# Attention with expert routing on one core: the first queries, a spread of maxima, a float32 key tile and a gate's transposes

## The chip, the cores and the metric

The kernel runs on one core of one Trainium2 chip. The metric is the device time of one execution in microseconds (us). TensorE is PE in the rows, its weight loads PEld, VectorE DVE, ScalarE ACT, GpSimd POOL and SyncE, which issues most transfers, SP.

## The reference

Attention with pooled queries, then a mixture of experts on its output. The routing is sequential over the tokens of a batch: a token keeps its predecessor's expert where a local gate says so.

```python
# q, k, v: (4, 8, 1152, 64) float32
q_pool = q.reshape(B, H, S // 2, 2, D).mean(axis=3)            # 576 queries a head
scores = scale * np.matmul(q_pool, k.transpose(0, 1, 3, 2))
scores = scores - np.max(scores, axis=-1, keepdims=True)
attn = np.exp(scores)
attn = attn / (np.sum(attn, axis=-1, keepdims=True) + 1e-09)
x = np.matmul(attn, v)                       # heads side by side: (4, 576, 512)
logits = x @ w_gate                          # 8 experts; local = sigmoid(x @ w_local)
e = argmax(logits) if s == 0 or local < 0.5 else e_of_the_token_before
out[b, s] = softmax(logits)[e] * (np.maximum(x @ w1[e], 0.0) @ w2[e])
```

## The kernel before

The 32 heads (4 batches of 8) are worked in 16 **pairs**, and each head in 9 **steps**, one for each tile of 128 keys: 288 steps `s`, 18 in a pair. Numbers are split into a high and a low 16-bit part, and products of the parts are added up in PSUM. The loop over `s` in `attention` writes the instructions in the order in which each engine runs them (the schedule is manual); what follows is what one turn of it issues.

- `scores(s)`: four products of 288 queries each (L227, L229) into a buffer `sc` (there are two), then one exponential on ScalarE (L231) into `ph`, float32.
- `feed_max(s)`: the maxima of the scores, which every exponential of a head needs ahead. A **unit** is a product of 512 or 128 columns into a buffer `psm` (L199, L201, L193; there are two) and a reduction of it on VectorE (L203, L194). An even head has 12 units (three of them, on the tile `QD`, for both heads' last 64 queries), an odd head 9. The list `when` sets the step from which a unit is issued: for head `n` it begins 13 steps before the head and ends within 9. After a head's last unit VectorE takes the maxima over units (L207), TensorE transposes them (L216), and ScalarE writes them as one row of `QA` (L217).
- `low(g)`: the low part of the exponentials, `ph` minus its upper half (L243), on GpSimd for even steps and for key tile 4 of a head, on VectorE for the other odd steps.
- `av(s - 6)`: the product with the values, six steps later. Where `F32K` names the key tile, it is five float32 products (L267), and there is no `low`; otherwise fifteen 16-bit ones (L269 to L271). `F32K` names tile 8 of every head and tile 4 of every odd head.
- `prep_ops(p)`: nine steps that make the 16-bit parts of pair p's keys, queries and values, spread over the steps from the 13th of pair p - 2: `kd` (L124, ScalarE), `qf` (L130, GpSimd), `qh` (L135, ScalarE), `kl` (L147) and `ql` (L153, GpSimd), `vt` (L163 ScalarE, L166 GpSimd), with transfers on SP that copy them to their places (`ks`, `qd`, `qs`, `qa`). Each SP transfer waits for its data at the head of one queue, in order. `load(p)` fetches `qf`, `kf` and `vf` of a pair into single buffers.
- `extra(s)`: weights of the experts. `WSTEPS` are 16 steps; 8 before one a transfer, 2 before it the high part (L526, ScalarE), at it the low part (L532, VectorE).
- After a batch's last head comes its **gate**, one small operation a step from the list `slow`: five transfers that transpose the attention output (`tr`, L562, on SP), the products of the logits (`logits2`, L600, TensorE), a chain of small VectorE operations (L606 to L703), and for batch 2 also `full_ops`. Between two transposes stand `nop` steps. An operation with a set of steps beside it waits until `s % 18` is in the set; for batch 2 that is `GPL2`, all but 4 and 8.

The start: pair 0 is prepared with some steps on VectorE (`first`), the units of head 0 are issued one after the other, each with a product whose result is not used (`warm`, L94), and then the loop begins. A copy of the last 64 queries of both heads into `QD` stands on VectorE there (L139). The preparation of pair 1 is issued from step 0 on, two operations a step. After the 288 steps come the last gate, the routing and eight phases of expert products.

```python
if first:
    V.tensor_copy(QD[i][r, r], qh[r, 512:576])          # L139
...
w = n * NKT - NKT - LEAD + (k * NKT) // nu              # L284, NKT 9, LEAD 4, nu 12 or 9
...
ts = [x for t in range(5) for x in [lambda t=t: tr(t, 8)] + [nop] * (NOP2 if b == B - 2 else 3)]   # L716, NOP2 2
```

## Time and profile before

| | us |
|---|---|
| median of three runs | 700.83 |
| lowest and highest | 698.24, 702.76 |
| the profiled execution | 698.33 |
| its span in the trace | 696.3 |

The profiled execution lies 2.5 us below the median, and 2.0 us of it lie around the span. Within the span the first exponential starts at 26.6 us, the 288 steps end near 438, and the rest is the last gate, the routing and the experts. A pair's stretch is counted below from the start of its first exponential to that of the next pair's. A row of a stretch has its bounds, its length, the busy time of PE, PEld, DVE, ACT and POOL with the number of instructions, the granted TensorE clock (1.00 is 2.4 GHz, 0.50 is 1.2 GHz), the busy share of the transfer engines and GB/s; the five rows of the first group are the pairs 0, 1, 3, 11 and 13.

### The profile page before, as it was taken

What the parts mean: (1) busy time and instruction counts of PE and PEld (TensorE: products, weight loads), DVE (VectorE), ACT (ScalarE), POOL (GpSimd) and SP (SyncE); (2) the same over time, 40 slices, a digit from 0 to 9 for tenths busy, and PEclk for the clock granted to TensorE, in tenths of its full rate; (3) what the DMA queues carried; (4) which work ended last, traced back from release to release, by engine and by line L of the source; (5) the groups of instructions that cost most, each with busy time, mean ns of one, the idle gap of its engine ahead of it and who ended that gap; (6) DMA issues with size and microseconds to landing.
All of it is one profiled execution on the core that took longest, in us unless ns stands there. A gap on an engine that the chain in (4) does not pass through costs nothing.

```text
span 696.3 us, 22820 instructions
## 1 busy us (share of the span) xinstructions
PE 647.7 (93%) x9214; PEld 504.7 (72%) x9214; DVE 594.8 (85%) x1084; ACT 426.7 (61%) x833; POOL 387.8 (56%) x346
## 2 busy tenths in 40 slices
PE   3799999999999999999997999979999999999994
PEld 0378778878888888887885778868649848848941
DVE  7778999999999999999986998578758899899952
ACT  2357777787776786777774666439785634643500
POOL 7477977977977887787794844558100000000073
PEclk9989999999999999999999999999999999999997
DMA  7365545648635748556574500838678877976762
GB/s 228 108 178 178 138 124 173 172 114 210 186 81 196 214 109 204 169 149 177 163 133 131 152 4 14 207 96 304 199 257 285 307 259 257 322 270 224 271 252 107
DMA packets 84221, 127.48 MB, mean 183 GB/s; under 512 B 37135, under 2 KB 43407, under 8 KB 84112
## 3 DMA queue, kind: packets, MB, share of 16 engines
q1 hardware_dynamic: 80912, 115.92, 55.1%
q0 software_dynamic: 3200, 10.05, 4.2%
q8 instruction: 76, 1.25, 0.7%
q14 instruction: 33, 0.27, 0.1%
HBM read 69.05 MB, written 10.04 MB: 114 GB/s over the span
## 4 chain that ended last, share of the span: by engine, by line
PE 46%; issue 27%; DVE 13%; DMA 4%; POOL 3%; ACT 3%; SPq 2%; POOLq 0%; DVEq 0%; ACTq 0%
PE sc L227 8%; PE sc L229 8%; PE psm L201 6%; PE av L267 6%; DVE mx L203 4%; PE av L270 4%; PE av L271 4%; PE av L269 4%; POOL out L1131 3%; DVE pl L243 2%; PE psm L199 1%; DVE w L532 1%; PE psh L216 1%; DMA xT<-xr 1%; DVE qd L139 1%
## 5 line engine op out<-in xcount | busy, mean ns | idle before, releaser
L231 ACT ACTIVATE ph<-sc 128x576 f32<-128x576 f32 x288 | 186.7, 649 | 101.5 <-PE sc L229 74.6
L203 DVE TENSOR_REDUCE mx<-psm 128x1 f32<-128x512 f32 (+1 forms) x300 | 193.1, 660 | 23.4 <-PE psm L201 21.5
L243 POOL TENSOR_TENSOR pl<-ph 128x576 f16<-128x576 f32 x128 | 174.6, 1374 | 15.1 <-ACT ph L231 15.1
L270 PE MATMUL av<-vt,ph 128*128 128x64 f16 x1200 | 136.0, 196 | 0.0
L269 PE MATMUL av<-vt,ph 128*128 128x65 f16 x1200 | 135.4, 193 | 0.0
L271 PE MATMUL av<-vt,pl 128*128 128x65 f16 x1200 | 135.1, 192 | 0.0
L243 DVE TENSOR_TENSOR pl<-ph 128x576 f16<-128x576 f32 x112 | 127.7, 1140 | 2.0 <-ACT ph L231 2.0
L270 PEld LDWEIGHTS <-ph 128*128 128x128 bf16 x1200 | 112.4, 98 | 21.9 <-issue 0.6
L269 PEld LDWEIGHTS <-ph 128*128 128x128 bf16 x1200 | 113.6, 98 | 16.6 <-issue 8.4
L227 PE MATMUL sc<-qs,ks 128*128 128x288 f16 x576 | 118.8, 288 | 0.8 <-ACT ph L231 0.7
L229 PE MATMUL sc<-qa,ks 65*128 65x288 f16 (+1 forms) x576 | 118.9, 288 | 0.3 <-ACT qa L217 0.3
L271 PEld LDWEIGHTS <-pl 128*128 128x128 f16 x1200 | 112.9, 100 | 0.0
...
L1127 PE MATMUL pso<-w,hq 128*128 x480 | 107.5, 380 | 0.0
L532 DVE SCALAR_TENSOR_TENSOR w<-wf,w 128x512 f16<-128x512 f32 x128 | 94.7, 747 | 13.8 <-ACT w L526 13.5
L201 PE MATMUL psm<-ks,qs 128*128 128x512 f16 x248 | 90.0, 384 | 7.3 <-DVE mx L203 7.2
L1116 PEld LDWEIGHTS <-wc 128*128 128x128 f16 x1728 | 87.7, 98 | 6.2 <-issue 4.4
L526 ACT ACTIVATE w<-wf 128x512 f16<-128x512 f32 x128 | 78.8, 631 | 18.8 <-DMA wf<-wq 17.9
L1127 PEld LDWEIGHTS <-hq 128*128 128x128 f16 (+1 forms) x576 | 45.8, 102 | 59.8 <-issue 11.7
L1116 PE MATMUL psh<-xr,wc 128*128 128x128 f16 (+1 forms) x1584 | 84.0, 211 | 2.3 <-DVE wc L984 1.1
L1225 POOL TENSOR_TENSOR xr<-xf,xr 128x320 f16<-128x320 f32 x30 | 35.5, 1182 | 61.1 <-PE sc L229 46.7
L229 PEld LDWEIGHTS <-ks 65*128 65x128 f16 (+1 forms) x576 | 56.8, 99 | 15.6 <-issue 0.6
...
## 6 DMA issues: line engine op xcount, KB each, us to landing
wf<-wq SPq DMA_DIRECT2D x128, 256.0 KB, 4.4
...
```

What stands on the lines that cost most here:

```text
L201: T.matmul(m[:, 0:w], q[:, t * 128:t * 128 + 128], k[:, c * 512:c * 512 + w], start=True, stop=True)
L203: V.tensor_reduce(out=mx[:, i, c:c + 1], in_=m[:, 0:w], op=ALU.max, axis=AX.X)
L227: T.matmul(sc[:, c, 0:288], ksl, QS[p][:, j, c * 288:(c + 1) * 288], start=True, stop=False)
L229: T.matmul(sc[:, c, 0:288], kal, QA[p % 3][u, j, c * 288:(c + 1) * 288], start=False, stop=True)
L231: A.activation(out=PHI[g % NPH][:, r * Q:(r + 1) * Q].rearrange("p (c q) -> p c q", c=2), in_=sc[:, :, 0:288], func=AF.Exp, scale=1.0 / 16)
L243: x.tensor_tensor(out=PLO[g % NPH][:, r * Q:r * Q + Q], in0=pf, in1=top(pf), op=ALU.subtract)
L269: T.matmul(o, ph[:, c:c + 128], v[:, j, kv, 0:65], start=(kt == 0 and t == 0), stop=False, skip_group_check=True)
L270: T.matmul(o[:, 0:64], ph[:, c:c + 128], v[:, j, kv, 65:129], start=False, stop=False, skip_group_check=True)
L271: T.matmul(o, pl[:, c:c + 128], v[:, j, kv, 0:65], start=False, stop=(kt == NKT - 1 and t == 4), skip_group_check=True)
L532: self.nc.vector.scalar_tensor_tensor(out=lo, in0=t, scalar=float(2 ** (W2S if ph % 2 else W1S)), in1=hi, op0=ALU.mult, op1=ALU.subtract)
L1116: self.nc.tensor.matmul(p[:, ft, c], u[:, ws, kk, ft * 128:ft * 128 + 128], x[:, 2 * kk + xs_, c], start=(n == 0 and ft == 0 and i == 0), ...
L1127: self.nc.tensor.matmul(p[c], h(hs, ft)[:, c], u(ws, ft), start=(first and n == 0), stop=(last and n == e), skip_group_check=(m < 128))
```

## The change

- At the start the copy into `QD` of pair 0 is ScalarE's, behind `qh` and ahead of `kd`. The transfers to `QD` stand ahead of those to `qs` for all pairs.
- VectorE clears part of `pl`, and TensorE multiplies those zeros eight times with nothing waiting for the result, ahead of its first unit.
- The queries of pair 1 are requested ahead of pair 0's low parts on SP, its keys and values after them, and its preparation is issued before step 0.
- `when`: the 21 units of a pair are spread over 18 steps.
- Key tile 4 of an odd head is float32 in the pairs 5, 6, 9, 10, 13 and 14 alone; in the ten others it is three 16-bit products, and GpSimd makes its low part.
- `WSTEPS`: two parts each in the pairs 1, 2, 3, 4, 8, 12 and four in pair 15 (before: two each in 2, 3, 4, 5, 8, 9, 11, 12).
- The gate's weights are split by ScalarE and GpSimd, no longer VectorE.
- Batch 2's gate: its five transposes are issued in one step, its logits wait for a step with `s % 18` of 9, and a `nop` stands between two later operations.

```diff
-F32K = ((8,), (4, 8))
+F32K1 = (5, 6, 9, 10, 13, 14)
+NWARM0 = 8
...
+        if part == 1:
+            SP.dma_start(out=ST[p][0], in_=kT[b, h:h + 2].rearrange("h d n -> (h d) n"))
+            load_v(p)
+            return
...
+    def in_f32(n, kt):
+        return kt == 8 or (kt == 4 and n % 2 == 1 and n // 2 in F32K1)
...
                 if first:
-                    V.tensor_copy(QD[i][r, r], qh[r, 512:576])
+                    A.activation(out=QD[i][r, r], in_=qh[r, 512:576], func=AF.Copy)
...
-            w = n * NKT - NKT - LEAD + (k * NKT) // nu
-            when.append(max(w, 0) if n == 1 else w)
+            if n == 0:
+                w = (k * NKT) // nu - NKT - LEAD
+            elif n == 1:
+                w = max(k - 2, 0) * 5 // 7
+            else:
+                w = n // 2 * 18 - 14 + (k + n % 2 * 12) * 18 // 21
+            when.append(w)
...
+    V.memset(PLO[0][:, 0:512].bitcast(F32), 0.0)
     load(0)
     load_v(0)
     load_ident()
+    for _ in range(NWARM0):
+        warm(PLO[0])
...
+    load(1, 0)
     rest = first[3:]
     for s in range(-NKT - LEAD, 0):
         feed_max(s)
         if s < 0 and rest:
             rest.pop(0)()
-        if len(rest) == 3 and 1 not in ST:
-            load(1)
+        elif s < 0 and prep:
+            prep.pop(0)()
+        if len(rest) == 3 and not prep:
+            load(1, 1)
+            prep += prep_ops(1)
...
-WSTEPS = [18 * t + o for t in (2, 3, 4, 5, 8, 9, 11, 12) for o in (0, 14)]
+WSTEPS = [18 * t + o for t in (1, 2, 3, 4, 8, 12) for o in (0, 14)] + [270 + o for o in (5, 8, 11, 14)]
+GPL1 = {9}
-NOP2 = 2
...
-        ts = [x for t in range(5) for x in [lambda t=t: tr(t, 8)] + [nop] * (NOP2 if b == B - 2 else 3)]
-        return [], None, ts + [(f, GPL2 if b == B - 2 else GPL) for f in [lambda: (logits2(0, 4), lcopy()), o1a, ...
+        ts = [lambda: [tr(t, 8) for t in range(5)]] if b == B - 2 else [x for t in range(5) for x in [lambda t=t: tr(t, 8)] + [nop] * 3]
+        gp = GPL2 if b == B - 2 else GPL
+        return [], None, ts + [(lambda: (logits2(0, 4), lcopy()), GPL1 if b == B - 2 else gp)] + [(f, gp) for f in [o1a, ...
```

ScalarE from its first work to the first exponentials, before (`qh`, `kd`, `vt_133` are pair 0's parts, `qa_130` the row of its maxima; the second `kd`, `qh` and `vt_134` are pair 1's):

```order
L135 ACTIVATE qh<-qf 128x576
L124 ACTIVATE kd<-kf 128x576
L163 ACTIVATE vt_133<-vf 128x2x4x64 x2
L217 ACTIVATE qa_130<-psh,pb 1x576
L231 ACTIVATE ph_143<-sc 128x576
L124 ACTIVATE kd<-kf 128x1152
L231 ACTIVATE ph_143<-sc 128x576
L135 ACTIVATE qh<-qf 128x576
L231 ACTIVATE ph_144<-sc 128x576 x2
L163 ACTIVATE vt_134<-vf 128x2x4x64 x2
```

The same stretch of ScalarE now (line numbers are those of the changed kernel):

```order
L143 ACTIVATE qh<-qf 128x576
L147 ACTIVATE qd_138<-qh 64x64 x2
L132 ACTIVATE kd<-kf 128x576
L173 ACTIVATE vt_133<-vf 128x2x4x64 x2
L132 ACTIVATE kd<-kf 128x1152
L227 ACTIVATE qa_130<-psh,pb 1x576
L143 ACTIVATE qh<-qf 128x576
L173 ACTIVATE vt_134<-vf 128x2x4x64 x2
L241 ACTIVATE ph_143<-sc 128x576 x2
```

Pair 1's `kd` now stands ahead of the row of maxima, and its `qh` and `vt` ahead of the first exponential. SP at the start, before:

```order
L143 DMA qs<-qh 64x576 x4
L127 DMA ks_129<-kd 64x2x1152 x2
L156 DMA qa_130<-ql 64x576 x2
L149 DMA ks_129<-kl 64x1152
L150 DMA ks_129<-kl 64x1152
L70 DMA qf_232<-qeo 128x1152
L73 DMA kf<-kT 128x1152
L80 DMA vf<-vL 128x2x576
```

And now:

```order
L153 DMA qs<-qh 64x576 x4
L135 DMA ks_129<-kd 64x2x1152 x2
L75 DMA qf_223<-qeo 128x1152
L166 DMA qa_130<-ql 64x576 x2
L159 DMA ks_129<-kl 64x1152
L160 DMA ks_129<-kl 64x1152
L69 DMA kf<-kT 128x1152
L88 DMA vf<-vL 128x2x576
```

Only the request for pair 1's queries has moved forward; keys and values still follow the low parts of pair 0. SP around batch 2's transposes, in the pairs 12 and 13, before:

```order
L86 DMA vx_137<-vL 128x64 x3
L562 DMA_TRANSPOSE xT<-xr 128x8x128
L127 DMA ks_128<-kd 64x2x1152 x2
L141 DMA qd_140<-qh 64x64
L143 DMA qs<-qh 64x576 x2
L141 DMA qd_140<-qh 64x64
L143 DMA qs<-qh 64x576 x2
L562 DMA_TRANSPOSE xT<-xr 128x8x128
L149 DMA ks_128<-kl 64x1152
L150 DMA ks_128<-kl 64x1152
L156 DMA qa_132<-ql 64x576 x2
L562 DMA_TRANSPOSE xT<-xr 128x8x128 x2
```

And now:

```order
L94 DMA vx_137<-vL 128x64
L584 DMA_TRANSPOSE xT<-xr 128x8x128 x5
L135 DMA ks_128<-kd 64x2x1152 x2
L149 DMA qd_140<-qh 64x64 x2
L153 DMA qs<-qh 64x576 x4
L159 DMA ks_128<-kl 64x1152
L160 DMA ks_128<-kl 64x1152
L166 DMA qa_132<-ql 64x576 x2
L75 DMA qf_7404<-qeo 128x1152
```

All five transposes stand ahead of pair 14's parts; before, the fifth stood behind the loads of pair 15, which follow these rows. VectorE where pair 3's even head takes over (`rc` belongs to the head before, `w_76` is a weight's low part), before:

```order
L207 TENSOR_REDUCE mn_141<-mx 128x5
L203 TENSOR_REDUCE mx<-psm 128x1
L1213 TENSOR_SCALAR rc<-av 128x5
L532 SCALAR_TENSOR_TENSOR w_76<-wf,w_76 128x512
L203 TENSOR_REDUCE mx<-psm 128x1
L1216 RECIPROCAL rc<-rc 128x5
L203 TENSOR_REDUCE mx<-psm 128x1
L243 TENSOR_TENSOR pl_152<-ph_147 128x576
L203 TENSOR_REDUCE mx<-psm 128x1 x2
L532 SCALAR_TENSOR_TENSOR w_76<-wf,w_76 128x512
```

And now:

```order
L217 TENSOR_REDUCE mn_141<-mx 128x5
L213 TENSOR_REDUCE mx<-psm 128x1
L1236 TENSOR_SCALAR rc<-av 128x5
L554 SCALAR_TENSOR_TENSOR w_76<-wf,w_76 128x512
L213 TENSOR_REDUCE mx<-psm 128x1
L1239 RECIPROCAL rc<-rc 128x5
L213 TENSOR_REDUCE mx<-psm 128x1 x2
L253 TENSOR_TENSOR pl_152<-ph_147 128x576
L213 TENSOR_REDUCE mx<-psm 128x1 x2
L554 SCALAR_TENSOR_TENSOR w_76<-wf,w_76 128x512
```

The weight's low part has kept its place beside `rc`; one reduction more stands between the two weight parts.

## Rows read from the trace of the kernel before

**Rows 1.** Busy times (instructions) by stretch, the pairs 0, 1, 3, 11 and 13.

```profile
26.60:54.10 27.50, 24.04 (x295) 17.91 (x294) 22.61 (x37) 17.70 (x31) 21.73 (x16) 0.88 0.57 154
54.10:79.50 25.40, 24.09 (x363) 20.01 (x360) 23.01 (x36) 18.87 (x38) 21.01 (x18) 1.00 0.50 142
...
104.50:129.50 25.00, 24.30 (x366) 20.24 (x365) 24.12 (x37) 19.20 (x40) 21.02 (x17) 1.00 0.51 150
...
306.60:332.00 25.40, 24.55 (x371) 20.44 (x370) 24.30 (x49) 19.22 (x38) 19.63 (x16) 1.00 0.65 196
...
357.00:389.50 32.50, 27.38 (x411) 22.40 (x409) 24.07 (x46) 19.22 (x39) 22.30 (x18) 0.95 0.59 133
```

**Rows 2.** Chain of waits in pair 3: start us, us, engine and line.

```profile
105.84 1.06 PE av L267 x10
...
107.61 0.03 PE av L269
...
108.07 0.24 PE sc L227 x2
...
124.97 1.32 DVE w L532
```

**Rows 3.** Timeline of the start: start us, us, engine, instruction, idle before it.

```profile
6.24 7.25 DVE L139 COPY qd<-qh 64x64 f16<-64x64 f16 x2
...
8.42 1.15 ACT L163 ACTIVATE vt<-vf 128x512 f16<-128x512 f32 x2 [1.68 <-DMA vf<-vL]
...
13.63 0.58 PE L199 MATMUL psm<-kd,qd 128*128 128x512 f16 x1 [5.72 <-DVE qd L139]
...
14.15 0.45 SPq L73 DMA_DIRECT2D kf<-kT  x1
...
14.69 0.38 SPq L80 DMA_DIRECT2D vf<-vL  x1
...
25.13 0.73 ACT L217 ACTIVATE qa<-psh,pb 1x576 f16<-1x576 f16 x1 [15.56 <-PE psh L216]
...
26.59 0.65 ACT L231 ACTIVATE ph<-sc 128x576 f32<-128x576 f32 x1 [0.72 <-PE sc L229]
27.26 1.16 ACT L124 ACTIVATE kd<-kf 128x1152 f16<-128x1152 f32 x1
```

**Rows 4.** Lines L73 and L80 in the first 60 and 40 us: time to landing.

```profile
DMA to landing us min/median/max: 4.1/5.0/6.0
...
DMA to landing us min/median/max: 6.0/6.3/6.8
```

**Rows 5.** Timeline of pair 0, around the units of pair 1's last queries.

```profile
34.43 1.01 PE L199 MATMUL psm<-kd,qd 128*128 128x512 f16 x2 [2.69 <-DMA qd<-qh]
```

**Rows 6.** Groups of instructions by line: busy us, mean ns; idle before.

```profile
L243 POOL TENSOR_TENSOR pl<-ph 128x576 f16<-128x576 f32 x128 | 174.6, 1374 | 15.1 <-ACT ph L231 15.1
...
L243 DVE TENSOR_TENSOR pl<-ph 128x576 f16<-128x576 f32 x112 | 127.7, 1140 | 2.0 <-ACT ph L231 2.0
...
L515 DVE SCALAR_TENSOR_TENSOR wgh<-wgf,wgh 128x36 f16<-128x36 f32 x1 | 1.1, 1075 | 0.0
```

**Rows 7.** Timeline of VectorE in pair 1.

```profile
68.43 0.75 DVE L243 TENSOR_TENSOR pl<-ph 128x576 f16<-128x576 f32 x1
...
70.98 1.95 DVE L243 TENSOR_TENSOR pl<-ph 128x576 f16<-128x576 f32 x1
```

**Rows 8.** Timeline of pair 13: SP's last transpose and TensorE's logits.

```profile
367.52 2.34 SPq L562 DMA_TRANSPOSE xT<-xr  x1
...
374.80 1.12 PE L600 MATMUL wide<-wgh,xT 128*128 128x18 f16 x36 [4.51 <-DMA xT<-xr]
```

**Rows 9.** Two short stretches of pair 13, same columns as in the first group.

```profile
370.00:374.80 4.80, 0.29 (x12) 0.19 (x8) 0.95 (x2) 0.41 (x2) 0.00 (x0) 1.00 0.97 262
374.80:378.20 3.40, 3.40 (x58) 2.68 (x59) 1.04 (x3) 1.22 (x3) 0.12 (x1) 0.50 0.02 5
```

**Rows 10.** Timeline of pair 14: TensorE's wait in the gate.

```profile
396.23 0.18 PE L678 MATMUL wide<-oh,c 128*128 128x40 f16 x1 [0.84 <-DVE oh L674]
```

More of the change, by code (lines that the diff above doesn't have):

```diff
@@ L50, in attention @@
     VT = [lat.tile([128, 2, NKT - 1, 130], F16, name=f"vt{i}") for i in range(3)]
-    VX = [lat.tile([128, sum(map(len, F32K)), 65], F32, name=f"vx{i}") for i in range(2)]
+    VX = [lat.tile([128, 3, 65], F32, name=f"vx{i}") for i in range(2)]
     QD = [pers.tile([128, 128], F16, name=f"qd{i}") for i in range(3)]
@@ L63, in attention, with load @@
     KD, QS, QH, ST = {}, {}, {}, {}
-    def load(p):
+    def load(p, part=None):
         b, h = divmod(2 * p, H)
+        if part == 1:
+            SP.dma_start(out=ST[p][0], in_=kT[b, h:h + 2].rearrange("h d n -> (h d) n"))
+            load_v(p)
+            return
         kf = stg.tile([128, S], F32, name="kf", tag="kf")
@@ L70, in load @@
         SP.dma_start(out=qf2, in_=qeo[b, h:h + 2].rearrange("h d r n -> (h d) r n"))
+        if part == 0:
+            ST[p] = [kf, qf2, vf]
+            return
         ks = kT[b, h:h + 2].rearrange("h d n -> (h d) n")
@@ L83, in load_x, with warm @@
         b, h = divmod(2 * p, H)
-        for j in range(2):
-            for kt in F32K[j]:
-                SP.dma_start(out=VX[p % 2][:, vx_at(j, kt), 0:64], in_=vL[b, h + j, :, kt * D:kt * D + D])
-    def vx_at(j, kt):
-        return j * len(F32K[0]) + F32K[j].index(kt)
-    def warm():
+        SP.dma_start(out=VX[p % 2][:, 0:2, 0:64], in_=vL[b, h:h + 2, :, 8 * D:9 * D].rearrange("h p d -> p h d"))
+        if p in F32K1:
+            SP.dma_start(out=VX[p % 2][:, 2, 0:64], in_=vL[b, h + 1, :, 4 * D:5 * D])
+    def in_f32(n, kt):
+        return kt == 8 or (kt == 4 and n % 2 == 1 and n // 2 in F32K1)
+    def warm(x=None):
+        x = KD[0] if x is None else x
         m = ps_s.tile([128, 2, 512], F32, name="sc", tag="sc")
-        T.matmul(m[:, 0], KD[0][:, 0:128], KD[0][:, 0:512], start=True, stop=True)
+        T.matmul(m[:, 0], x[:, 0:128], x[:, 0:512], start=True, stop=True)
     def setup(i, W):
@@ L138, in o3 @@
                 if first:
-                    V.tensor_copy(QD[i][r, r], qh[r, 512:576])
+                    A.activation(out=QD[i][r, r], in_=qh[r, 512:576], func=AF.Copy)
                 else:
                     SP.dma_start(out=QD[i][r, r], in_=qh[r, 512:576])
+            for j in range(2):
+                r = slice(64 * j, 64 * j + 64)
                 for a in range(2):
@@ L239, in low @@
             n, kt = divmod(2 * g + r, NKT)
-            if kt not in F32K[n % 2]:
+            if not in_f32(n, kt):
                 x = V if r and kt != 4 else G
@@ L261, in av @@
         ph, pl = top(PHI[s // 2 % NPH]), PLO[s // 2 % NPH]
-        v, kv = VT[p % 3], kt
+        v = VT[p % 3]
         for t in range(5):
@@ L265, in av @@
             c = (s % 2) * Q + t * 128
-            if kt in F32K[j]:
-                T.matmul(o, PHI[s // 2 % NPH][:, c:c + 128], VX[p % 2][:, vx_at(j, kt)], start=False, stop=(kt == NKT - 1 and t == 4), skip_group_check=True)
+            if in_f32(n, kt):
+                T.matmul(o, PHI[s // 2 % NPH][:, c:c + 128], VX[p % 2][:, j if kt == 8 else 2], start=False, stop=(kt == NKT - 1 and t == 4), skip_group_check=True)
                 continue
-            T.matmul(o, ph[:, c:c + 128], v[:, j, kv, 0:65], start=(kt == 0 and t == 0), stop=False, skip_group_check=True)
-            T.matmul(o[:, 0:64], ph[:, c:c + 128], v[:, j, kv, 65:129], start=False, stop=False, skip_group_check=True)
-            T.matmul(o, pl[:, c:c + 128], v[:, j, kv, 0:65], start=False, stop=(kt == NKT - 1 and t == 4), skip_group_check=True)
+            T.matmul(o, ph[:, c:c + 128], v[:, j, kt, 0:65], start=(kt == 0 and t == 0), stop=False, skip_group_check=True)
+            T.matmul(o[:, 0:64], ph[:, c:c + 128], v[:, j, kt, 65:129], start=False, stop=False, skip_group_check=True)
+            T.matmul(o, pl[:, c:c + 128], v[:, j, kt, 0:65], start=False, stop=(kt == NKT - 1 and t == 4), skip_group_check=True)
         if kt == NKT - 1:
@@ L512, in gate_weights @@
     def gate_weights(self):
[L513 to L515 removed]
+        A, G = self.nc.scalar, self.nc.gpsimd
+        A.activation(out=self.wgf, in_=self.wgf, func=AF.Copy, scale=float(2 ** GS))
+        A.activation(out=self.wgh[:, :, 0], in_=self.wgf, func=AF.Copy)
+        G.tensor_tensor(out=self.wgh[:, :, 1], in0=self.wgf, in1=self.wgh[:, :, 0], op=ALU.subtract)
     def w_load(self, ph, c):
```

6 lines of the change are left out of this document (1 added, 5 removed).

## The prediction, made before the changed kernel ran

> **What bounds the kernel now.** I read four views in this order: the busy times by stretch, the chain of waits in one quiet pair, the timelines of the three places where TensorE stands still, and the groups of instructions by line. The stretches are cut at pairs, since a share over the whole span would mix the start, the attention and the experts. In a quiet pair, the third line of [rows 1], TensorE is busy for 24.30 of 25.00 us and VectorE for 24.12: two engines are full at once, and whichever is relieved, the other is 0.2 us behind it. ScalarE has 5.8 us to spare and GpSimd 4.0. The chain in that pair [rows 2] runs through TensorE's products for nearly all of its length, and through VectorE once, where a weight's low part takes 1.32 us while TensorE waits for a free `psm`. So a pair ends when TensorE has issued its products, plus one wait of some 0.7 us. Apart from that, TensorE stands still at three places: 5.72 us at the start [rows 3], 2.69 us in pair 0 [rows 5], 4.51 us in pair 13 [rows 8].
>
> **The change, part by part.** *The start.* VectorE's two copies into `QD` take 7.25 us, and the third unit waits 5.72 us for them until 13.63 [rows 3]. ScalarE would make them: the trace has no copy of 64 columns there, so its price lies between nothing and the 0.58 us of a half of `vt`, two of which take 1.15 [rows 3]; I take half, 0.3 each, as it has far fewer columns. They could begin where VectorE's began, at 6.24, and `QD` would be there at 6.8. The zero products come ahead: eight at 0.58, the length of a 512-column product at that time, are 4.6 us from about 2.5 on, when VectorE has cleared the tile, so they hold the first unit to about 7.1, and the third is issued near 8.2, 5.4 us earlier than 13.63. From there to the row of maxima L217 the trace takes 25.13 - 13.63 = 11.5 us, which would put it at 19.7.
>
> The engine ahead of that step is ScalarE, and the new order puts pair 1's `kd` in front of L217, and `qh` and `vt` behind it but ahead of the first exponential. These wait for transfers. Pair 1's keys are requested at 14.15, its values at 14.69, and that place in SP's queue stays where it was, since only the queries moved ahead. Keys land after 4.1 to 6.0 us, 5.0 in the middle [rows 4]: at 19.15, or 18.25 at the earliest. `kd` (1.16 us [rows 3]) then ends at 20.3, L217 (0.73) at 21.0, `qh` (taken like half of `vt`, 0.58) at 21.6, the values (6.3 after 14.69: 21.0) are there, `vt` (1.15) ends at 22.8, and the first exponential follows. With the earliest landing it is L217 that decides, at 19.7: 20.4, 21.0, 22.2. I take 22.6, which is 4.0 us earlier than 26.59. So of the 5.4 us, 1.4 are given back to the new wait; queued behind it on ScalarE are the exponentials, and TensorE's second scores wait for them. If the low clock of the start ended earlier thanks to the zeros, the units would come sooner, but not L217: I count nothing for that.
>
> *Pair 0.* It takes 27.50 us with VectorE busy for 22.61 [rows 1]. Its wait of 2.69 us for pair 1's `qd` [rows 5] goes, since the preparation now stands ahead of step 0, and the low clock that follows it (mean 0.88) with it. What is late next is VectorE: 22.61 plus the 0.88 that it idles in the quiet pair is 23.5. Gain 4.0, between 0 (nothing but the start moves) and 4.9 (VectorE without a pause).
>
> *Key tile 4.* Five float32 products hold TensorE for 1.06 us, fifteen 16-bit ones for 108.07 - 107.61 = 0.46 [rows 2]: 0.60 us less in ten pairs. GpSimd gets one low part more, 1.37 us [rows 6], in pairs where it has 4.0 to spare. Now VectorE is the bound: in the five pairs with two weight parts (2, 3, 4, 8, 12) TensorE needs 24.30 - 0.60 = 23.70, VectorE 24.12 as before. The spread of the maxima, 21 over 18 steps in place of 12 in one half and 9 in the other, takes no work away, but lets VectorE fall behind less. A pair can end between 24.1 (VectorE without a pause) and 25.0 (nothing gained); I take 24.5, a little over half of what is possible, since two full engines that share two buffers cannot both be without pauses. That is 0.5 each, 2.5 in sum. Pair 1 loses the gate weights' split from VectorE (two operations like L515, of 1.08 us [rows 6]) and gets two weight parts at up to 1.32: 23.01 - 2.2 + 2.6 = 23.4 on VectorE, 23.5 on TensorE; at 24.5 it gains 0.9. Pair 11 loses its two weight parts: VectorE 24.30 less 1.5 to 2.6, TensorE 24.55 - 0.60 = 23.95; at 24.3 it gains 1.1. Pair 7, as long, has no weight part to lose: 0.7. The pairs 5, 6, 9 and 10 keep their float32 tile and only lose weight parts and bunched maxima: 0.6 for the four together. The sum for the pairs 1 to 12 is 5.8. Pair 15 gets four weight parts more on a VectorE that is far from full there, and 0.60 less on TensorE: I count nothing.
>
> *Pair 13.* The logits of batch 2 stop for 4.51 us until the fifth transpose has landed, since SP issues it at 367.52 only [rows 8], behind pair 14's parts and pair 15's loads. During the stop the transfer engines are 0.97 busy, and the 3.40 us after it run at a granted clock of 0.50 [rows 9]. Now all five stand at the first one's place, 12 steps or more ahead of the logits, which stay at their step. That removes the 4.51 and, of the 3.40 at half the clock, up to 1.7. I take 6.0 for both. The price: five issues at 1.2 to 2.3 us each stand ahead of pair 14's `ks`, `qd` and `qs` on SP, some 4 us later than now; their first reader is 10 steps on, so I count nothing. In pair 14 the `nop` stands where TensorE waits 0.84 us for VectorE [rows 10]: 0.8.
>
> Sum: 4.0 + 4.0 + 5.8 + 6.0 + 0.8 = 20.6. The profiled execution had 698.33, so 677.7 for one like it; it lies 2.5 under the median of the three runs. I predict 678.5.
>
> **A rule against it.** A product on VectorE takes 0.75 us where GpSimd is idle and up to 1.95 where it works [rows 7], 1.14 in the mean [rows 6]; the low parts of both engines read two operands each from the same memory. The Trainium skill, SBUF — State Buffer, section "Who interferes with whom", says that a VectorE instruction with two SBUF inputs and a GpSimd instruction that reads SBUF exclude each other: whoever is first holds the ports to its end, and the other stands still. By that rule each of the ten added low parts could hold VectorE for its whole length; what that would cost is the first rival. The trace agrees with the rule so far as the two lengths of one product go.
>
> **The rivals.** *Exclusion* (0.07): the added 1.37 us on GpSimd lands on VectorE in full. VectorE then needs 24.12 + 1.37 = 25.5 us in each of the ten pairs: they lose 0.5 instead of gaining some 0.5, 10.2 us against the forecast: 688.7. For it speaks that VectorE's products are at 1.14 and not 0.75 in the mean, against it that GpSimd's 21.0 of 25 us already meet them and the added part mostly fills a gap in which VectorE reduces from PSUM.
>
> *TensorE's gain in full* (0.13): VectorE's products get shorter or overlap better, and ten pairs lose both the 0.60 and the 0.7 of waiting: 13 instead of 5.2, so 670.7. For it: the wait comes at one place in a pair, where the maxima were bunched. Against: VectorE has 24.12 us of work.
>
> *The start is held* (0.12): keys or values of pair 1 land at the late end or later, since the queries' transfer now goes among pair 0's parts; the first exponential starts at 25 and pair 0 is VectorE's with its pauses, 26.0. Then 1.6 + 1.5 remain of 8.0: 683.4.
>
> *The transposes are still late, or make pair 14's parts late* (0.05): TensorE stops at the logits as before, or ten steps on for `qd`, for 4.5 us: 683.
>
> *Slower* (0.03): with more GpSimd work behind every product, VectorE's seven low parts in a pair go from 1.14 to 1.6 us each; 24.12 + 3.2 = 27.3 in ten pairs, 2.3 more than now. That is 23 lost where I count 5.2 gained: 706.7. It decides from about 1.5 us on (VectorE 26.5 a pair), where the ten pairs eat the other 15.4 us. Rows of 1.95 speak for it, and that GpSimd has 4 us without work in each pair against it.
>
> **How the numbers follow.** The forecast has 0.60 and is the likeliest. Its own bounds come from the start (first exponential 22.2 to 22.8, pair 0 23.0 to 25.0), the pairs (4 to 8 us) and pair 13 (4.5 to 6.2): 674 to 683. The range of 671 to 687 takes in the second, third and fourth rival and leaves out the slower one and exclusion. One per cent, 7 us, is about what a measurement of this kernel can tell from no change. Faster by over 1% is below 693.8: all cases but the slower one, less a little for exclusion and a held start together: 0.94. Within 1% is that combination, 0.03; slower 0.03.
>
> **What the changed profile would show.** Right: no wait of TensorE on `qd` over 1 us at the start; `kd` of pair 1 ending just ahead of L217's place on ScalarE, and a first exponential near 22.6; pairs 2, 3, 4 and 12 at 24.5 with VectorE's idle time under 0.5; a pair 13 under 27 with no slow clock. Wrong: a first exponential after 25, quiet pairs at 25 or more, VectorE's products at 1.4 us in the mean, or a TensorE wait for `xT` or for pair 14's `qd`.

## The result and the profile after

The changed kernel takes 709.21 us in the median of four runs (707.34 to 711.40), the kernel before 699.88 in four runs beside it: ratio 1.013, 95% interval 1.0081 to 1.0179. I had forecast 678.5, and 687 as the upper bound. The profiled execution of the changed kernel had 711.40, the slowest of its four; its span is 709.3, 13.0 us above that of before, where the medians are 9.3 apart. The gains and losses by stretch below add up to the 13.0.

The lines moved by some ten: L231 is now L241 (exponentials), L243 is L253 (low parts), L203 and L194 are L213 and L204 (maxima), L199 and L201 are L209 and L211 (units), L193 is L203 (the last unit of a head), L532 is L554 (weights' low parts), L217 is L227.

Page of the changed kernel: the chain that ended last, and VectorE's low parts (busy us, mean ns).

```profile
DVE 34%; issue 28%; PE 26%; POOL 4%; ACT 3%; DMA 3%; SPq 0%; POOLq 0%; ACTq 0%; DVEq 0%
...
L253 DVE TENSOR_TENSOR pl<-ph 128x576 f16<-128x576 f32 x112 | 143.2, 1279 | 0.0
```

VectorE's 112 low parts grew from 1140 to 1279 ns [rows 6], though nobody gave them more elements, and VectorE has the largest share of the chain. Busy times by stretch say where the time went: first the pairs 1 to 12 in one row, then the pairs 0, 3, 6 and 8, a part of pair 8, and the pairs 13, 14 and 15.

```profile
48.40:370.54 322.14, 302.34 (x4531) 243.65 (x4530) 297.30 (x480) 225.65 (x453) 254.91 (x201) 0.98 0.55 147
23.47:48.40 24.93, 22.99 (x288) 16.99 (x286) 21.19 (x37) 15.84 (x28) 20.00 (x26) 0.92 0.61 173
98.75:125.44 26.69, 24.36 (x370) 19.48 (x369) 25.59 (x37) 18.95 (x39) 22.25 (x18) 1.00 0.47 140
177.82:205.47 27.65, 26.21 (x380) 21.03 (x379) 25.67 (x49) 18.86 (x38) 20.28 (x17) 1.00 0.45 119
231.94:263.61 31.67, 28.70 (x370) 22.62 (x369) 26.53 (x41) 18.82 (x38) 21.36 (x17) 0.84 0.46 121
240.00:249.50 9.50, 9.50 (x76) 7.30 (x74) 5.57 (x9) 3.09 (x6) 2.84 (x3) 0.51 0.40 130
370.54:397.87 27.33, 25.82 (x415) 20.79 (x414) 24.92 (x48) 19.33 (x40) 23.52 (x19) 1.00 0.56 154
397.87:425.74 27.87, 26.12 (x381) 20.99 (x380) 25.82 (x52) 16.80 (x35) 14.48 (x13) 1.00 0.29 92
425.74:448.60 22.86, 20.60 (x363) 18.38 (x362) 21.53 (x46) 16.02 (x36) 12.22 (x10) 1.00 0.23 39
```

The same stretch of twelve pairs in the kernel before:

```profile
54.09:357.04 302.95, 296.48 (x4489) 246.91 (x4486) 288.90 (x486) 228.09 (x455) 250.06 (x193) 1.00 0.57 161
```

The start, pair 0 and pair 13 gained 3.1, 2.6 and 5.2 us, 10.9 of the 14.0 forecast. The pairs 1 to 12 lost 19.2 where I had them gain 5.8: 25 of the 31 us by which the forecast was off. VectorE's busy time in these pairs grew by 8.4 us, with 480 instructions in place of 486. Pair 8, at 31.67 us, has a stretch at the low clock; pair 12, which has the same waits of TensorE and no such stretch, takes 27.09, so some 4.6 of the 19.2 are that clock. Pair 15 lost 1.7. From the start of the last exponential to the end of the span it was 260.7 us (709.3 less 448.6) against 257.8; this part lay between 256.3 and 266.4 in the kernels below, and I didn't pursue it.

One place of pair 3 shows what a loss looks like: timeline of the changed kernel, steps 1 to 5.

```profile
100.55 1.14 POOL L253 TENSOR_TENSOR pl<-ph 128x576 f16<-128x576 f32 x1
100.57 1.67 DVE L554 SCALAR_TENSOR_TENSOR w<-wf,w 128x512 f16<-128x512 f32 x1
...
102.16 1.28 DVE L213 TENSOR_REDUCE mx<-psm 128x1 f32<-128x512 f32 x2
...
103.19 1.14 POOL L253 TENSOR_TENSOR pl<-ph 128x576 f16<-128x576 f32 x1
...
103.36 1.58 DVE L253 TENSOR_TENSOR pl<-ph 128x576 f16<-128x576 f32 x1
...
104.86 0.68 DVE L204 TENSOR_REDUCE mx<-psm 128x4 f32<-128x512 f32 x1
...
105.60 0.38 PE L209 MATMUL psm<-kd,qd 128*128 128x512 f16 x1 [1.15 <-DVE mx L204]
```

GpSimd's low part begins at 103.19 and ends at 104.33; VectorE's, begun 0.17 us later, ends at 104.94, 0.61 after it. The weight part at 100.57 ends at 102.24, 0.55 after GpSimd's that began just before it (101.69). Behind these two stand the reductions, and TensorE, which issues in order, waits 1.15 us at L209 for a `psm` buffer, with scores and values queued behind. An instruction that stands until GpSimd's has ended, as these two of VectorE do, is called held below.

### The profile page after: what moved, and what is told of

Its sections match the earlier page's. It is cut to its first block, busy times and chain, and to the rows that moved or that the text cites. A ratio compares the mean times of both kernels' runs of the same rounds, so it can differ in the third digit from the quotient of the medians.

```text
span 709.3 us, 22905 instructions
## 1 busy us (share of the span) xinstructions
PE 654.6 (92%) x9272; PEld 502.8 (71%) x9272; DVE 603.5 (85%) x1081; ACT 427.6 (60%) x837; POOL 394.6 (56%) x357
## 4 chain that ended last, share of the span: by engine, by line
DVE 34%; issue 28%; PE 26%; POOL 4%; ACT 3%; DMA 3%; SPq 0%; POOLq 0%; ACTq 0%; DVEq 0%
DVE mx L213 13%; DVE pl L253 11%; PE psm L211 4%; PE sc L237 4%; PE sc L239 4%; PE av L277 3%; POOL out L1154 3%; DVE w L554 2%; DVE mx L204 2%; PE av L280 2%; PE av L281 2%; PE av L279 2%; DMA gkf<-xs,gid 1%; POOL pl L253 1%; PE psh L226 1%
## 5 line engine op out<-in xcount | busy, mean ns | idle before, releaser
L241 ACT ACTIVATE ph<-sc 128x576 f32<-128x576 f32 x288 | 187.0, 651 | 97.8 <-PE sc L239 81.7
L213 DVE TENSOR_REDUCE mx<-psm 128x1 f32<-128x512 f32 (+1 forms) x300 | 191.0, 658 | 34.1 <-PE psm L211 33.1
L253 POOL TENSOR_TENSOR pl<-ph 128x576 f16<-128x576 f32 x138 | 187.1, 1365 | 31.8 <-ACT ph L241 31.8
L253 DVE TENSOR_TENSOR pl<-ph 128x576 f16<-128x576 f32 x112 | 143.2, 1279 | 0.0
L280 PE MATMUL av<-vt,ph 128*128 128x64 f16 x1250 | 141.6, 195 | 0.0
L279 PE MATMUL av<-vt,ph 128*128 128x65 f16 x1250 | 141.0, 193 | 0.0
L281 PE MATMUL av<-vt,pl 128*128 128x65 f16 x1250 | 140.7, 192 | 0.1
L279 PEld LDWEIGHTS <-ph 128*128 128x128 bf16 x1250 | 118.2, 97 | 29.1 <-issue 22.9
L280 PEld LDWEIGHTS <-ph 128*128 128x128 bf16 x1250 | 117.1, 98 | 24.9 <-issue 0.8
L237 PE MATMUL sc<-qs,ks 128*128 128x288 f16 x576 | 119.7, 290 | 1.5 <-DVE oh L696 0.8
L281 PEld LDWEIGHTS <-pl 128*128 128x128 f16 x1250 | 117.5, 99 | 0.3 <-POOL pl L253 0.2
L554 DVE SCALAR_TENSOR_TENSOR w<-wf,w 128x512 f16<-128x512 f32 x128 | 96.6, 762 | 13.9 <-ACT w L548 13.2
L211 PE MATMUL psm<-ks,qs 128*128 128x512 f16 x248 | 93.4, 388 | 14.0 <-DVE mx L213 7.1
L1150 PEld LDWEIGHTS <-hq 128*128 128x128 f16 (+1 forms) x576 | 45.8, 102 | 59.8 <-issue 11.7
L1248 POOL TENSOR_TENSOR xr<-xf,xr 128x320 f16<-128x320 f32 x30 | 27.3, 911 | 57.8 <-ACT xr L1245 57.8
```

What stands on the lines that cost most here:

```text
L211: T.matmul(m[:, 0:w], q[:, t * 128:t * 128 + 128], k[:, c * 512:c * 512 + w], start=True, stop=True)
L213: V.tensor_reduce(out=mx[:, i, c:c + 1], in_=m[:, 0:w], op=ALU.max, axis=AX.X)
L237: T.matmul(sc[:, c, 0:288], ksl, QS[p][:, j, c * 288:(c + 1) * 288], start=True, stop=False)
L241: A.activation(out=PHI[g % NPH][:, r * Q:(r + 1) * Q].rearrange("p (c q) -> p c q", c=2), in_=sc[:, :, 0:288], func=AF.Exp, scale=1.0 / 16)
L253: x.tensor_tensor(out=PLO[g % NPH][:, r * Q:r * Q + Q], in0=pf, in1=top(pf), op=ALU.subtract)
L279: T.matmul(o, ph[:, c:c + 128], v[:, j, kt, 0:65], start=(kt == 0 and t == 0), stop=False, skip_group_check=True)
```

## The experiments

"The old spread" means that from head 2 on the list `when` is that of before. The last column is the stretch of the pairs 1 to 12 in each profile. The theories are named in the expectations.

| kernel | median us | ratio to before, 95% interval | pairs 1 to 12, us |
|---|---|---|---|
| changed | 709.21 | 1.013 (1.0081 to 1.0179) | 322.1 |
| 1 old spread | 690.18 | 0.9842 (0.9806 to 0.9878) | 301.2 |
| 2 float32 tile in all | 706.33 | 1.0078 (1.0052 to 1.0104) | 319.5 |
| 3 start and gates alone | 689.32 | 0.9831 (0.979 to 0.9873) | 304.1 |
| 4 before, spread alone | 715.84 | 1.0224 (1.0184 to 1.0264) | 318.9 |
| 5 doubles at odd steps | 707.18 | 1.0101 (1.0063 to 1.014) | 317.0 |
| 6 no GpSimd low parts | 685.11 | 0.9787 (0.9758 to 0.9816) | 298.8 |
| 7 the same, old spread | 678.38 | 0.9672 (0.9636 to 0.9709) | 290.2 |
| 8 as 3, doubles at odd steps | 703.57 | 1.0051 (1.0027 to 1.0075) | 317.4 |
| 9 low parts a step later | 706.36 | 1.008 (1.0049 to 1.0112) | 317.8 |
| 10 the same, old spread | 708.43 | 1.0094 (1.0063 to 1.0126) | 324.0 |
| 11 as 3, low parts a step later | 706.81 | 1.0096 (1.0064 to 1.0128) | 322.2 |
| 12 as 1, no low part of tile 4 | 688.27 | 0.9822 (0.9786 to 0.9858) | 299.5 |
| 13 gates' step 8 for 3 | 706.82 | 1.0078 (1.005 to 1.0106) | 317.4 |
| 14 as 1, no zero products | 690.81 | 0.9841 (0.9788 to 0.9894) | 301.2 |
| 15 as 1, float32 in 8 and 12 | 692.2 | 0.9856 (0.9804 to 0.9907) | 302.1 |
| 16 no weight low parts | 699.06 | 0.9982 (0.9951 to 1.0013) | 311.1 |
| 17 weights at 7 and 13 | 702.87 | 1.0032 (1.0004 to 1.006) | 313.8 |
| 18 as 1, weights at 7 and 13 | 687.12 | 0.9794 (0.9746 to 0.9842) | 298.3 |

### Which part of the change: the spread

Kernel 1 has the first edit, kernel 2 the second, kernel 3 all three; kernel 4 puts the new line into the kernel before.

```diff
-                w = n // 2 * 18 - 14 + (k + n % 2 * 12) * 18 // 21
+                w = n * NKT - NKT - LEAD + (k * NKT) // nu
...
-F32K1 = (5, 6, 9, 10, 13, 14)
+F32K1 = tuple(range(16))
...
-WSTEPS = [18 * t + o for t in (1, 2, 3, 4, 8, 12) for o in (0, 14)] + [270 + o for o in (5, 8, 11, 14)]
+WSTEPS = [18 * t + o for t in (2, 3, 4, 5, 8, 9, 11, 12) for o in (0, 14)]
```

> The changed kernel with one thing undone: from head 2 on the maxima are issued from the steps that they had before (12 units of the even head in nine steps, 9 of the odd head in nine). Theory S (the even spread of the maxima is what puts VectorE behind): pairs 2 to 12 go back to 25.0 us or below, VectorE's low parts from 1.28 us in the mean to about 1.14, and the time falls by some 20 us to 685 to 690. Theory X (the added low part on GpSimd lands on VectorE): pairs 2, 3, 4, 7, 8, 11, 12 stay at 25.7 us or more, the mean stays above 1.22 us, and the time is 703 to 709.

> The changed kernel with key tile 4 of every odd head in float32 again, as before; the spread of the maxima and the rest as changed. Theory S: the pairs that had no float32 tile are about as long as the pairs 5, 6, 9 and 10 are in the changed kernel, 25.3 to 27.7 us, and the time stays at 704 to 712. Theory X: those ten pairs lose about 1.4 us of VectorE each and the time is 690 to 696.

> The changed kernel with spread of the maxima, key tile 4 and steps of the weights' low parts all as before; the start, the gate's weights and batch 2's gate as changed. By the two traces these three gave 3.1 us at the start, 2.6 in pair 0 and 5.2 in pair 13. Both theories: 700 less 11, 687 to 691, with pairs 2 to 12 at their lengths of before (24.7 to 25.9 us). If it is above 695, something that neither theory names, such as the order of the preparation or of the transfers, costs time in the pairs.

> The kernel before with one thing changed: from head 2 on the maxima stand evenly over 18 steps. Theory S: pairs 2 to 12 grow by 0.5 us or more each, VectorE's low parts pass 1.2 us in the mean, and the time is 706 to 720. Theory X: 698 to 702, no change.

All four times came out as theory S has them (kernel 1 is 0.2 us above its range). Not all lengths did: in kernel 1 the pairs 6, 8, 10 and 12 still took 25.4 to 25.7 us and VectorE's low parts 1.17 in the mean, and in kernel 3 the pairs 5, 9, 10 and 11 took 26.1 to 26.2. Kernel 1, pairs 1 to 12, pair 3 and pair 6:

```profile
49.02:350.22 301.20, 293.23 (x4515) 240.82 (x4514) 285.62 (x480) 224.59 (x452) 258.05 (x200) 1.00 0.58 157
97.77:122.65 24.88, 23.96 (x370) 19.52 (x369) 24.09 (x37) 18.98 (x39) 22.50 (x18) 1.00 0.51 151
172.62:198.03 25.41, 25.38 (x378) 20.92 (x375) 24.82 (x48) 18.90 (x39) 20.56 (x17) 1.00 0.45 131
```

Kernel 4, the same three:

```profile
52.23:371.13 318.90, 302.06 (x4491) 246.30 (x4490) 295.60 (x486) 227.77 (x454) 245.51 (x192) 1.00 0.56 153
104.62:130.53 25.91, 24.80 (x365) 20.18 (x364) 24.38 (x37) 19.18 (x39) 20.76 (x17) 1.00 0.49 145
183.42:211.08 27.66, 26.21 (x380) 21.03 (x379) 25.54 (x49) 18.88 (x38) 20.14 (x17) 1.00 0.43 121
```

The spread costs 19 us on the changed kernel and 15 on the one before. GpSimd's added low part can't be the cause: without it (kernel 2) the time stays at 706. Between the changed kernel and kernel 1 the twelve pairs differ by 20.9 us; VectorE is busy for 11.7 of them (297.30 less 285.62), and idles for the other 9.2. What it costs TensorE stands in its waits in these pairs (us in total, times, longest), for the changed kernel and then for kernel 1:

```profile
PE psm L209 <- DVE mx L204: 6.5, 9, 1.2
PE psm L211 <- DVE mx L213: 6.3, 17, 0.8
PE psm L203 <- DVE mx L213: 3.3, 4, 1.4
PE psm L209 <- DVE mx L213: 1.8, 4, 0.5
```

```profile
PE psm L211 <- DVE mx L213: 5.2, 8, 0.9
PE psm L209 <- DVE mx L204: 1.4, 5, 0.4
PE psm L209 <- DVE mx L213: 0.6, 3, 0.2
```

TensorE waits 17.9 us for reductions with the spread and 7.2 without it: 10.7 of the 20.9 us. Pair 8's low clock is some 4.6 more.

### Why: held instructions or the order of the units

```diff
-                w = n // 2 * 18 - 14 + (k + n % 2 * 12) * 18 // 21
+                w = n // 2 * 18 - 14 + ((k + n % 2 * 12) * 18 + 3) // 21
```

This is kernel 5, and kernel 8 with the float32 tile and `WSTEPS` of before. Kernels 6 and 7 (old spread) leave low parts out; the `pl` tiles are set to zero once.

```diff
-            if not in_f32(n, kt):
-                x = V if r and kt != 4 else G
+            if r and kt != 4 and not in_f32(n, kt):
+                x = V
```

> The changed kernel with the same even spread, but three of a pair's 21 units one step later, so that the steps with two units are 5, 11 and 17 of a pair's 18 in place of 4, 10 and 16. At even steps VectorE also has a low part, which in its order stands behind the reductions; at odd steps it has none. Theory P (two reductions and a low part in one step are what VectorE can't do in time): pairs 2 to 12 go back to 25.2 us or less, and the time is 684 to 692. Theory E (an even spread costs time wherever its doubles stand, because it moves all reductions against GpSimd's work): 700 to 710.

> The changed kernel without GpSimd's low parts: those of the even steps and of key tile 4 are left out, and zeros stand in their place, so that the products that read them are those of before in number and shape. Theory H (VectorE's low part is held by GpSimd's instruction, and that is what the spread makes worse): VectorE's low parts take about 0.75 to 0.85 us, pairs 2 to 12 fall to 23.5 to 24.5 us, and the time is within 4 us of that of the same kernel with the old spread. Theory O (the order alone: units that wait for one of two buffers behind two reductions): it stays 10 us or more above that one.

> The counterpart: the changed kernel with the spread of before from head 2 on, and without GpSimd's low parts in the same way. Both theories: VectorE is relieved and TensorE is the bound, 23.2 to 24.3 us in a pair, 670 to 682 us. What tells the theories apart is the distance between these two kernels, 19 us with GpSimd's low parts: below 4 by theory H, 10 or more by theory O.

> Start, gate's weights and batch 2's gate as changed, float32 tile and weights' steps as before, and the even spread with its doubles at 5, 11 and 17. Theory P: the spread then costs nothing against the 689.3 us of the kernel that has the old spread in its place, 684 to 691. Theory E: 703 or more.

Kernels 5 and 8 lie in theory E's ranges, so theory P fell, but not in every pair. Kernel 5, pairs 1 to 12, 3 and 6:

```profile
49.40:366.38 316.98, 298.47 (x4521) 242.85 (x4518) 283.98 (x480) 224.44 (x453) 255.41 (x199) 0.99 0.56 149
98.73:123.95 25.22, 24.10 (x369) 19.56 (x369) 23.41 (x38) 19.07 (x38) 22.48 (x18) 1.00 0.51 149
174.27:204.07 29.80, 27.54 (x379) 22.02 (x379) 26.11 (x50) 19.03 (x39) 20.67 (x17) 0.94 0.42 113
```

Pair 3 went from 26.69 to 25.22, near the 24.88 of the old spread; pair 6, which holds a gate's operations, from 27.65 to 29.80, a part of it at the low clock (0.94 in the mean). Kernels 6 and 7, pairs 1 to 12:

```profile
48.91:347.73 298.82, 293.79 (x4531) 240.59 (x4530) 251.19 (x480) 226.29 (x453) 121.90 (x97) 1.00 0.59 159
```

```profile
47.97:338.18 290.21, 290.21 (x4520) 241.34 (x4518) 252.99 (x480) 224.15 (x453) 120.47 (x97) 1.00 0.61 163
```

Low part of VectorE in kernel 6, from its page:

```profile
L253 DVE TENSOR_TENSOR pl<-ph 128x576 f16<-128x576 f32 x112 | 94.5, 844 | 0.4 <-ACT ph L241 0.3
```

Without GpSimd's low parts VectorE's take 0.84 us in the mean in place of 1.28, and the spread costs 6.7 us and not 19 (8.6 in the twelve pairs and not 20.9). So some 12 us of the loss are there only together with GpSimd's low parts, the 4.6 of pair 8's low clock among them, and 7 to 9 come from the order of the units alone, with VectorE no busier under the spread than without: in the twelve pairs TensorE has waits of 4.6 us in kernel 6 and none in kernel 7. Neither theory had that number (below 4, or 10 or more): both are at work. These runs remove GpSimd's work as well as the hold, so the split is not one of pure mechanisms.

### VectorE's low parts one step later

```diff
-            if s > 0 and s % 2 == 0:
-                low(s // 2 - 1)
+            if s > 1:
+                low(s // 2 - 1, V if s % 2 else G)
```

`low` then issues only the parts of the engine that it is given.

> The changed kernel, even spread and all, with VectorE's low parts issued one step later, an odd step behind GpSimd's of the same pair of steps; GpSimd's stay where they are. Theory H (the spread made VectorE's low parts start just behind GpSimd's, so that each waits to the end of GpSimd's): VectorE's low parts fall from 1.28 us in the mean to 1.0 or less, and the time from 709 to 685 to 695. Theory O (the order of units alone): 703 or more. If the low parts keep their length because they now meet GpSimd's other work, the time says nothing for either.

> The same shift of VectorE's low parts by one step in the kernel that has the old spread, 690.2 us without it. Theory H: with the low parts at 1.0 us or less in place of 1.17, VectorE has some 1.2 us less in a pair and TensorE is the bound: 680 to 687. If the old spread's low parts already meet GpSimd's work no more than the shifted ones do, 688 to 695.

> The same shift in the kernel with spread, float32 tile and weights' steps as before (689.3 us without it). TensorE needs 0.6 us more in ten pairs than in the kernel with key tile 4 in 16 bit, and GpSimd one low part less: by theory H 684 to 689, and above the other shifted kernel by 2 to 5; without theory H 688 to 694.

Kernel 9 came out in theory O's range: the low parts fell to 1.14 us only, above theory H's 1.0, and the time by 2.9. The expectations for kernels 10 and 11 were wrong: 18 to 21 us above theory H's ranges and 13 above the others. The low parts did get shorter: 1.28 to 1.14 in kernel 9, 1.17 to 1.12 in kernel 10 and 1.14 to 1.02 in kernel 11. Yet the two kernels with the old spread lost 18 and 17 us. Kernel 10, pairs 3, 6 and 8:

```profile
96.84:121.73 24.89, 24.04 (x370) 19.62 (x369) 23.13 (x37) 19.09 (x39) 22.73 (x18) 1.00 0.53 151
172.44:199.96 27.52, 25.66 (x378) 20.99 (x375) 25.90 (x48) 19.00 (x39) 20.59 (x17) 1.00 0.44 124
227.27:258.31 31.04, 27.42 (x370) 21.72 (x369) 25.60 (x41) 18.96 (x38) 20.65 (x17) 0.89 0.45 120
```

Pair 3 is as it was (24.88), VectorE even 1.0 us less busy; pairs 6 and 8 lose 2 and 5, in pair 8 with a part at the low clock (0.89 in the mean). Timeline of kernel 10 in pair 6:

```profile
177.14 1.11 DVE L253 TENSOR_TENSOR pl<-ph 128x576 f16<-128x576 f32 x1
...
178.18 1.11 DVE L647 TENSOR_TENSOR t<-t,c 128x40 f32<-128x40 f32 x1
...
179.21 0.68 DVE L204 TENSOR_REDUCE mx<-psm 128x4 f32<-128x512 f32 x1
...
179.94 0.38 PE L209 MATMUL psm<-kd,qd 128*128 128x512 f16 x1 [1.10 <-DVE mx L204]
```

A gate's product of 40 elements takes 1.11 us behind GpSimd, and it stands with the moved low part right ahead of the last reduction of a head, for which TensorE waits 1.10. So the mean of the low parts doesn't set the time by itself; in this pair it is what stands ahead of a reduction that TensorE waits for.

### Key tile 4, the zeros, the gates' steps

Kernel 12 skips GpSimd's low part at key tile 4 of odd heads, kernel 13 changes one number of the gates' list, kernel 14 has no zero products, kernel 15 two more pairs with the float32 tile. The kernels 12, 14 and 15 have the old spread, as kernel 1.

```diff
-            if not in_f32(n, kt):
+            if not in_f32(n, kt) and (kt != 4 or n % 2 == 0):
...
-GPL = {0, 1, 3, 7, 9, 13, 14, 15, 17}
+GPL = {0, 1, 7, 8, 9, 13, 14, 15, 17}
...
-NWARM0 = 8
+NWARM0 = 0
...
-F32K1 = (5, 6, 9, 10, 13, 14)
+F32K1 = (5, 6, 8, 9, 10, 12, 13, 14)
```

> The kernel with the old spread (690.2 us), in which GpSimd's low part for key tile 4 of the odd heads is left out in the ten pairs that have it (the products read what an earlier step left there). If the added part holds VectorE, as theory H has it, the pairs 3 and 4 fall from 24.9 to 24.5 us or less and the time by 3 to 6, to 684 to 687. If it is hidden in GpSimd's spare time, pairs and time stay: 689 to 691.

> The changed kernel, even spread and all, with one number of the gate's list of steps changed for batches 0 and 1: step 8 in place of step 3. Theory G (a gate's operation released at step 3 runs on VectorE just ahead of the two reductions of step 4, held by GpSimd's low part, 1.06 us in place of 0.2, and TensorE waits for those reductions): pairs 6, 7, 10 and 11 lose 0.6 us or more each, pairs 8 and 12 their waits at steps 4 and 5, and the time falls by 4 to 10 us, to 699 to 705. If the reductions are late there anyway, 707 to 711.

> The changed kernel with the old spread from head 2 on (690.2 us) without the eight products of zeros at the start. My prediction counted nothing for the zeros, since pair 1's keys hold the first exponential: 689 to 691, first exponential within 0.5 us of 23.5. The rival: without them the first units run at the low clock and the maxima of head 0 come later than the keys: first exponential at 25 or more, 692 to 694.

> The kernel with the old spread (690.2 us) with key tile 4 in float32 in the pairs 8 and 12 too, which have two weight parts each. If the added low part on GpSimd is what makes these pairs slow (25.7 us, 24.8 where they have the float32 tile), each falls by 0.5 to 1.0 and the time is 688 to 689.5; if it is their weight parts, no change, 690 to 691.

In kernel 12 pair 3 takes 24.99 us, not less than the 24.88 with the part: it is hidden there. The median is 1.9 lower, between the two ranges expected and with overlapping intervals, and the pairs 8 and 12 are where it comes from. Pair 8 of kernel 1, then of kernel 12:

```profile
223.27:248.95 25.68, 23.64 (x359) 19.06 (x356) 24.76 (x40) 18.60 (x38) 22.03 (x18) 1.00 0.52 144
225.45:250.27 24.82, 23.62 (x364) 19.20 (x361) 23.91 (x40) 18.67 (x38) 20.68 (x17) 1.00 0.55 151
```

Pair 12 falls alike, 25.7 to 24.8. Kernel 15, which leaves the part out in these two pairs alone, is no faster (692.2, above both ranges expected): they take 25.8 there. Whether it is the pair ahead of them whose part counts, no run tells. Kernel 14 has its first exponential at 23.66: the zeros give no time. With them a product of 512 columns takes 0.38 us from 7.4 us on (0.61 or more in kernel 14), but TensorE then stands idle for 3.91 us, and from 18.2 to 23.5 us its granted clock is 0.50, where kernel 14 has 1.00. Kernel 13, pairs 6, 8 and 10:

```profile
177.81:205.90 28.09, 26.06 (x380) 21.04 (x379) 25.64 (x48) 18.85 (x39) 21.18 (x17) 1.00 0.48 122
232.05:258.38 26.33, 24.35 (x370) 19.49 (x369) 25.07 (x41) 18.56 (x39) 21.77 (x18) 1.00 0.46 134
285.43:312.00 26.57, 25.11 (x370) 20.49 (x369) 23.36 (x45) 18.85 (x38) 19.71 (x16) 1.00 0.43 123
```

Of its 4.7 us in the twelve pairs pair 8 alone gave 5.3, most of it the low clock; pair 10 won 1.1, pair 9 lost 1.4 and pair 6 0.4. The time lies between the two ranges expected, and one step of the gates is not what makes those pairs dear.

### The weights' low parts

Kernel 16 lets ScalarE write a copy in their place, 17 and 18 move them.

```diff
+        if ph == 0 and c < 12:
+            return self.nc.scalar.activation(out=lo, in_=t, func=AF.Copy)
...
-for t in (1, 2, 3, 4, 8, 12) for o in (0, 14)]
+for t in (1, 2, 3, 4, 8, 12) for o in (7, 13)]
```

> The changed kernel, even spread and all, in which the low parts of the weights of pairs 1, 2, 3, 4, 8 and 12 are not computed: ScalarE writes a copy into their place, so that VectorE has two operations less in each of those pairs. Theory L (the even spread puts two more units into the half of a pair in which VectorE has the weights' low parts): pairs 2, 3, 4, 8 and 12 fall from 25.7 to 26.7 us (31.7 in pair 8) to 25.2 or less, and the time by 8 us or more, to 701 or less. If their lengths come from the held low parts of the exponentials alone, they stay above 25.5 and the time is 702 to 707.

> The changed kernel with the weights' low parts at steps 7 and 13 of their pairs in place of 0 and 14 (transfers and high parts move with them). In the changed kernel's trace GpSimd has no work at VectorE's low part of step 7, so a weight part there would take 0.7 to 0.8 us and not 1.5. Theory L: pairs 3 and 4 fall by 0.8 us or more, 700 to 705. If the place is of no account: 707 to 711.

> The same places for the weights' low parts in the kernel with the old spread (690.2 us). By theory L steps 5 to 13 are the full half there, 12 units: TensorE waits more at steps 6 to 9, and the time is 690 to 695. If only GpSimd's hold counts, the parts get shorter by 0.7 us each and the time falls to 684 to 688.

Kernel 16, pairs 3 and 6, then kernel 17, pair 3:

```profile
97.27:121.91 24.64, 23.87 (x370) 19.50 (x369) 21.68 (x34) 19.89 (x42) 21.83 (x18) 1.00 0.52 153
172.52:200.19 27.67, 26.22 (x380) 21.04 (x379) 25.45 (x49) 18.88 (x38) 19.96 (x17) 1.00 0.43 118
```

```profile
98.66:123.80 25.14, 24.06 (x370) 19.48 (x369) 22.96 (x37) 19.25 (x39) 22.33 (x18) 1.00 0.52 150
```

Theory L holds for the pairs 2, 3 and 4: pair 3 falls from 26.69 to 24.64 without the weight parts and to 25.14 when they are moved. The pairs 8 and 12 stay at 26.5 without them. Kernel 17 doesn't tell room from hold, since the two parts take 0.96 and 0.83 us in their new places and took 1.67 and 1.27 in the old. Pair 6, with a gate and no weights, stays at 27.67 and 27.66. In kernel 18, where theory L had 690 to 695, the time is 3.1 us below kernel 1's, in the range of the reading by which only the hold counts, and the lowest median of the kernels that compute everything, though the intervals overlap. But its weight parts got shorter by 0.3 and 0.2 us in pair 3 (1.77 to 1.47, 1.27 to 1.10) and not by 0.7 each, so that reading isn't shown either.

## Why the prediction was wrong, point by point

**The pairs 1 to 12**: forecast 5.8 gained, measured 19.2 lost. The step that failed reads: "The spread of the maxima ... takes no work away, but lets VectorE fall behind less. A pair can end between 24.1 ... and 25.0". The upper end, 25.0 (nothing gained), was taken as a bound, though no row excluded a loss. Two things were wrong in it. First, VectorE's 24.12 us of [rows 1] are not all work: they contain time in which an instruction is held by GpSimd, and that depends on where it starts against GpSimd's: in the changed kernel's trace 92 of the 112 low parts begin while GpSimd is in a product of its own, in kernel 1's 76. The rows to see it were there ([rows 7]: 0.75 and 1.95 for the same product), but the sum had VectorE's low parts at their mean, whatever the order. Second, the old spread left room: it had 9 units in steps 14 to 4, where the weights' parts and most of the gates' steps stand, and 12 in the others. The new one put two more units there. Kernels 1 and 4 show that the spread alone is the loss, and TensorE's waits that half of it is TensorE standing still for late reductions. Kernels 6 and 7 show that some 12 of the 20.9 us need GpSimd's low parts, and 16 that in the pairs 2, 3 and 4 it is the spread together with the weights' parts. Why the pairs 6, 7, 10 and 11 lose 1.2 to 2.2 us each against kernel 1 is not settled: the timelines show a gate's operation held ahead of a reduction, but moving one of its steps (kernel 13) didn't cure it.

**Key tile 4**: of 0.60 us less on TensorE I took about half as gain. With the old spread, pair 3 gained 0.1 (24.99 to 24.88), though TensorE's busy time fell by 0.32 (24.28 in kernel 3, 23.96 in kernel 1). VectorE stayed at 24.09; that it was the bound there is likely, but no run shows it. Kernels 1 and 3 differ by 0.9 us in the median, within both intervals. By the first rival VectorE would have needed 25.5 us there, so it falls too; what the low part on GpSimd does cost is seen in the pairs 8 and 12 alone (kernel 12), 0.9 us each.

**The start**: forecast 4.0, measured 3.1. The mechanism was as forecast. Timeline of ScalarE in the changed kernel:

```profile
19.78 1.16 ACT L132 ACTIVATE kd<-kf 128x1152 f16<-128x1152 f32 x1 [10.26 <-DMA kf<-kT]
20.97 0.73 ACT L227 ACTIVATE qa<-psh,pb 1x576 f16<-1x576 f16 x1
...
23.47 1.42 ACT L241 ACTIVATE ph<-sc 128x576 f32<-128x576 f32 x2
```

`kd` waits 10.26 us for pair 1's keys and L227 stands behind it, as said; the keys landed 0.6 later than the 19.15 that I took. That zeros count for nothing in the time was right (kernel 14).

**Pair 0**: forecast 23.5, measured 24.93. The wait for `qd` is gone as forecast, but VectorE, with 21.19 us, is not "late next" in the way that I summed it: TensorE waits 1.5 us for reductions, at `psm` and L226. The low clock stayed too (0.92 in the mean), but it doesn't set the length: with the old spread pair 0 takes 25.80 us at 0.94 (kernel 1) and 25.81 at 1.00 (kernel 14). With VectorE's low parts a step later it takes 23.7 (kernels 10 and 11; 24.8 in kernel 9), so the order on VectorE has a part in it; the rest is open.

**Pair 13**: forecast 6.0, measured 5.2; TensorE has no wait for `xT` and no slow clock, and five issues take 8.01 us on SP without making pair 14 wait. **Pair 14**: forecast 0.8, measured a loss of 0.1: TensorE waits for the same product with L237 in place of L678. **Pair 15**: counted at nothing, lost 1.7; 1.5 of these are there in kernel 3, which has the moved gate and not the four weight parts. Kernel 8 has the moved gate too and takes 21.28, 0.1 more than before, so the gate alone doesn't make them either; the cause is open.

**The slower rival** gave 706.7, close to the time, and by the sign it foresaw VectorE's longer products. But it had them come from more GpSimd work, at 1.6 us; they came to 1.28, and from the spread. Its number is near by luck.
